# x transposed by DMA, and every segment 320 matmuls long, in a recurrent-memory attention and gMLP kernel

## The chip, the cores and the metric

The kernel runs on one core of one Trainium2 chip. What counts is the time of one execution on the device, in microseconds (us). Times of the kernel are medians of several executions; the views of the profile come from one profiled execution.

## What is computed

Two blocks follow one another. Block A is attention over 64 segments of 32 rows, in order: each segment's input is 8 memory rows and 32 rows of the normalised x, and the first 8 output rows are the memory of the next segment. Block B is a gMLP block over all 2048 rows. Cut to what matters here:

```python
for s in range(n_seg):                       # 64 segments, one after the other
    xs = x[:, s*32:(s+1)*32, :]              # x is layernorm(A_x), 2048 x 512
    h = concatenate([mem, xs], axis=1)       # 8 + 32 rows
    q, k, v = h @ Wq, h @ Wk, h @ Wv         # 32 heads of 128
    p = softmax(mask(q @ k.T * scale))
    o = (p @ v) @ Wo
    mem = o[:, :8, :]                        # goes on to segment s + 1
    outs.append(o[:, 8:, :])
h = A_x + concatenate(outs)
z = gelu(layernorm(h) @ w_in)                # 2048 x 1792
g = w_sp @ layernorm(z[..., 896:]) + b_sp    # mixes the rows
out = h + (z[..., :896] * g) @ w_out
```

All inputs are bfloat16.

## The kernel before

**How it is written.** Each instruction is added in Python to one of five lists, one for each engine: `pe` (TensorE, PE below), `act` (ScalarE), `dve` (VectorE), `pool` (GpSimd), and `sp` (SyncE, which issues DMAs). An engine works through its list in order. The writer names what an instruction reads and writes, and the class `Emitter` puts in the waits between engines; a wait that is already implied by an earlier one is left out. One wait rides on an instruction; where there are two, the second stands in the queue as an instruction of its own. An access to a bank of PSUM is tracked bank by bank, so a write to a bank waits until the other engines have read what stood there.

**A pair.** Each matmul is two instructions of PE's queue, the load of its weights and the matmul itself; below this is a pair. Nearly all of block A is written as groups of four pairs that fill the four 32-column strips of the array side by side (`tile_position=(0, 32 * c)`).

**Two parts of a segment.** PE doesn't multiply 40 rows at once. The recurrent part, 24 rows of x and the 8 of memory, goes through segment by segment. The last 8 rows of x of each segment don't fit into the 32 columns; they are worked out ahead of time for 16 segments together (a chunk): their Q and K columns (`qkx_mm`) and their V (`vx_mm`, whose result is stored to memory and loaded segment by segment as `Vx`). Their output projection is done for four segments together (`WoX_mm`, 8 pairs for each quarter), and scattered into rows by `WoX_scatter`.

**The loop over segments** (lines 975 to 1139), with `rb = s // 4`, the row block of 128 rows, and `j4 = s % 4`. What PE does from the first score matmul of a segment to that of the next one, in pairs:

- scores of the first half of the heads (20), V of the first half (16), scores of the second half (20), sums of the softmax and V of the second half in turns (8, 12, 8, 4)
- a column group `xs` of 16 pairs for a later chunk (lines 1056 to 1061): until segment 47 Q, K or V columns, from segment 49 on a part of z for block B
- an atom of a V group: four pairs of a group of 16, from the stock `gv` (class `Gap`; `gv.pour(n)` gives up to n atoms, and ends early where a group is complete, so that its result can be copied out)
- P times V (20 + 20), which needs the normalised E of DVE
- `WoX_mm` of the row block before (8, from the second row block on)
- Wo (56), the first half of the memory output `mem_out(s, 0)` (8), the rest of Wo (8)
- where j4 is 0 the residual rows (`F_group`, 4), where it is 3 `WoX_scatter` (4), where it is 2 the transposes of x described below (16), where it is 1 the second half of WoX, or an atom
- Q and K of the next segment: 8 pairs that need the first half of the memory columns, `mem_out(s, 1)` (8), and the other 72

The memory columns come to the next segment over PE (`mem_out`), ACT (line 724 copies them from bank `GB` = 1 into `hT`) and back to PE (`QK`). In `pour`, the number of atoms for a segment comes from `nC`: 3 in the first row block, then 2 for j4 = 1 and 1 otherwise.

**x.** `load_x(rb + 2, 0)` loads a row block two row blocks ahead, for j4 = 0; `ln_inplace(0)` normalises it for j4 = 1; for j4 = 2 PE transposes it with 16 matmuls against the identity (`xT_cols`, line 392) into PSUM bank `FBK`, and ACT copies it into a ring of 12 segment slots, `hT` (`ring_copy`, line 402), from which Q, K and V read. Segment 3 transposes 128 rows more, for the last chunk.

**Other queues.** SP issues, in its order, the loads of x and of the residual, the stores of V columns, `load_vx(s + 2)` (Vx for two segments later), pieces of the transposed w_sp (`wT_piece`, in odd segments) and, from segment 47 on, the transposes by DMA of the rows that block B needs (`xn2T_dma`, line 788). At the end of segment 47 it issues the load of one half of w_in. POOL copies the extra columns of Q (`qx_copy`, line 559, for the next segment), multiplies the small part of E (line 630), copies columns of cT (`cTx_copy`) and works out the reciprocal roots of the layernorms (`rstd`). `S_half` waits for POOL's `qx_copy` and for DVE at its first pair, so there the second wait stands by itself in PE's queue, in three segments of four.

**Start.** Before the first real work PE runs 78 small matmuls on a constant tile of ones (line 826) and some larger ones (`warm`).

## Time and profile before

| what | us |
|---|---|
| time, median of 3 executions | 849.89 (849.73 to 851.56) |
| the profiled execution | 849.45 |
| its span, from the first to the last instruction | 847.7 |
| PE busy in it | 832.2 |
| ACT busy | 498.4 |
| DVE busy | 493.3 |
| POOL busy | 154.8 |

How to read it: PE's busy time is the union of its matmuls, whose ends are modelled and which overlap (the mean matmul of 512 columns in line 534 is given 380 ns, though 3072 of them take 185.2 us together). A PE that is busy may therefore still stand behind its best pace; the pace is read from the starts of successive rows. In rows of the timeline the columns are start, length from the first start to the last end, engine, line, operation, shapes, count, and in brackets the idle time before with what ended it; "issue" means that nothing the profile shows was waited for. Rows of the chain of waits have start, length and what ran. Rows that group instructions have busy time, mean ns of one, and the idle time before. Rows of a window have its bounds, its length, then the busy time and count of PE, PEld (weight loads), DVE, ACT and POOL, the granted PE clock (1.00 throughout), the DMA share and GB/s; a window's count includes matmuls that are still in flight at its start.

### The profile page before, as it was taken

How to read it: one execution, taken by the hardware profiler on the slowest of the kernel's cores; microseconds unless marked ns; L12 is line 12 of the kernel's file. 1: busy time of each engine (PE TensorE's matmuls, PEld its weight loads, DVE VectorE, ACT ScalarE, POOL GpSimd, SP SyncE). 2: the span in 40 equal slices, each digit the busy share in tenths (PEclk: the TensorE clock that was granted, in tenths of full speed). 3: DMA queues.
4: the chain of work that ended last, by engine and by line, in shares of the span. 5: the costliest groups of instructions: out<-in, count | busy, mean ns of one | idle time of the engine just before them, and what ended most of it. 6: DMA issues, size and time to landing. Idle time of an engine off the chain costs nothing.

```text
span 847.7 us, 48032 instructions
## 1 busy us (share of the span) xinstructions
PE 832.2 (98%) x22034; PEld 475.2 (56%) x22034; DVE 493.3 (58%) x1175; ACT 498.4 (59%) x1419; POOL 154.8 (18%) x409
## 2 busy tenths in 40 slices
PE   8999999999999999999999999999999999999997
PEld 8655555555555555555556556555655544444443
DVE  4446556666565656565656566566656576553443
ACT  3456677767676777667777777666666676300000
POOL 5212111112211111111222121112211123200000
PEclk9999999999999999999999999999999999999999
DMA  9972222120301130213212130523332389023101
GB/s 330 386 216 87 70 45 62 52 78 21 82 29 44 57 79 29 66 59 61 65 30 77 30 79 26 122 70 77 70 82 59 70 268 305 1 99 100 44 13 46
DMA packets 95359, 76.03 MB, mean 90 GB/s; under 512 B 46184, under 2 KB 80624, under 8 KB 95152
## 3 DMA queue, kind: packets, MB, share of 16 engines
q1 hardware_dynamic: 93232, 70.09, 28.8%
q8 instruction: 174, 2.85, 1.5%
q10 hardware_dynamic: 1648, 2.49, 0.9%
q0 software_dynamic: 272, 0.33, 0.1%
q14 instruction: 33, 0.27, 0.1%
HBM read 41.75 MB, written 20.91 MB: 74 GB/s over the span
## 4 chain that ended last, share of the span: by engine, by line
PE 93%; DMA 3%; SPq 2%; issue 1%; ACT 0%; DVE 0%; POOL 0%; POOLq 0%
PE f_ps L534 27%; PE f_ps L701 14%; PE f_ps L640 13%; PE f_ps L1206 11%; PE f_ps L422 4%; PE f_ps L746 4%; PE f_ps L1301 3%; PE f_ps L472 3%; PE f_ps L665 2%; PE f_ps L797 2%; PE f_ps L1199 2%; PE f_ps L445 2%; DMA f_arena<-in_A_Wo_dram 1%; PE f_ps L585 1%; SPq L884 1%; PE f_ps L606 1%
## 5 line engine op out<-in xcount | busy, mean ns | idle before, releaser
L534 PE MATMUL f_ps<-f_arena,f_hT 128*32 128x512 bf16 (+1 forms) x5120 | 241.3, 337 | 0.9 <-ACT f_part L713 0.5
L534 PEld LDWEIGHTS f_ps<-f_arena,f_hT 128*32 128x32 bf16 x5120 | 117.2, 96 | 99.7 <-ACT f_hT L724 34.2
L545 ACT ACTIVATE f_Tst<-f_ps 128x512 bf16<-128x512 f32 (+2 forms) x320 | 146.7, 511 | 32.8 <-PE f_ps L534 32.1
L640 PE MATMUL f_ps<-f_arena,f_hT 128*32 128x512 bf16 x2048 | 138.7, 379 | 0.0
L701 PE MATMUL f_ps<-f_arena,f_cT 128*32 128x256 bf16 x4096 | 134.6, 273 | 1.2 <-issue 0.5
L630 POOL TENSOR_TENSOR f_E_sb<-f_R_sb,f_E_sb 128x64 bf16<-128x64 f32 x128 | 47.2, 369 | 387.1 <-ACT f_R_sb L622 386.5
L701 PEld LDWEIGHTS f_ps<-f_arena,f_cT 128*32 128x32 bf16 x4096 | 95.8, 95 | 31.8 <-ACT f_cT L687 8.8
L652 DVE TENSOR_SCALAR f_V_sb<-f_ps 128x512 bf16<-128x512 f32 (+1 forms) x128 | 71.4, 558 | 54.2 <-PE f_ps L640 54.2
L1206 PE MATMUL f_ps<-f_arena 128*128 128x512 bf16 x448 | 100.6, 379 | 0.1
L553 DVE STREAM_TRANSPOSE f_QT<-f_Tst 128x256 uint32<-128x256 uint32 x128 | 57.1, 446 | 65.6 <-ACT f_Tst L545 60.9
L689 DVE TENSOR_SCALAR f_cT<-f_ps 128x320 bf16<-128x320 f32 x128 | 56.8, 486 | 40.7 <-PE f_ps L671 40.7
L713 ACT ACTIVATE f_part<-f_ps 128x256 bf16<-128x256 f32 x128 | 49.2, 384 | 41.0 <-PE f_ps L701 38.9
L1206 PEld LDWEIGHTS f_ps<-f_arena 128*128 128x128 bf16 x448 | 43.6, 98 | 52.7 <-DMA f_arena<-wT_d 0.3
L687 ACT ACTIVATE f_cT<-f_ps 128x160 bf16<-128x160 f32 (+1 forms) x192 | 53.8, 346 | 26.5 <-PE f_ps L671 26.5
L599 ACT ACTIVATE f_E_sb<-f_ps 128x224 bf16<-128x224 f32 x128 | 45.4, 355 | 39.2 <-PE f_ps L611 39.2
L553 DVE STREAM_TRANSPOSE f_KT<-f_Tst 128x256 uint32<-128x256 uint32 (+2 forms) x192 | 60.7, 342 | 5.7 <-ACT f_Tst L545 3.0
L640 PEld LDWEIGHTS f_ps<-f_arena,f_hT 128*32 128x32 bf16 x2048 | 46.0, 95 | 20.0
L724 ACT ACTIVATE f_hT<-f_ps 128x16 bf16<-128x16 f32 x126 | 23.2, 184 | 47.7 <-PE f_ps L721 47.7
L571 DVE CAST f_ps<-f_mask 128x224 f32<-128x224 bf16 x80 | 29.8, 372 | 35.3 <-ACT f_hT L402 32.4
L1212 DVE TENSOR_TENSOR f_arena<-f_ps,f_arena 128x512 f32<-128x512 f32 x28 | 19.3, 689 | 52.7 <-PE f_ps L1206 52.7
L622 ACT ACTIVATE f_R_sb<-f_R_sb 128x160 f32<-128x160 f32 x128 | 43.1, 337 | 4.4 <-ACT f_Vs L484 0.4
L746 PE MATMUL f_ps<-f_arena,f_cTx 128*32 128x512 bf16 x512 | 41.5, 383 | 0.0
(128 smaller groups left out, 1142.0 us busy)
## 6 DMA issues: line engine op xcount, KB each, us to landing
wT_d<-f_wst SPq DMA_DIRECT2D x32, 256.0 KB, 2.3
f_arena<-wT_d SPq DMA_DIRECT2D x32, 256.0 KB, 5.0
f_arena<-in_A_Wv_dram SPq DMA_DIRECT2D x4, 1024.0 KB, 13.1
f_arena<-in_A_Wk_dram SPq DMA_DIRECT2D x4, 1024.0 KB
f_arena<-in_A_Wo_dram SPq DMA_DIRECT2D x4, 1024.0 KB, 12.3
f_Vx<-vext_d SPq DMA_DIRECT2D x62, 64.0 KB
vext_d<-f_Vs SPq DMA_DIRECT2D x22, 128.0 KB, 2.7
zp_d<-f_Vs SPq DMA_DIRECT2D x20, 112.0 KB, 1.7
```

The lines of the kernel that those rows point to most:

```text
L534: pe(lambda e, dc=dc, c=c, rhs=rhs: e.matmul(ps[32 * c:32 * c + 32, bank, 0:32 * nh], lhsT=hT[:, sl, dc, :], rhs=rhs, start=(dc == 0), sto ...
L545: act(lambda e: e.activation(out=st_.rearrange("p (hp i r) -> p hp i r", i=32, r=2), in_=ps[:, bank, 0:64 * np_].rearrange("p (hp r i) -> ...
L553: dve(lambda e: e.transpose(out=dst, in_=src), reads=tok, writes=[(nm, b, k) for k in halves(b, p0, np_)])
L630: pool(lambda e: e.tensor_tensor(out=ev, in0=rv, in1=ev, op=ALU.mult), reads=[("R", b), ("Ex", b)], writes=[("Ex", b)])
L640: pe(lambda e, dc=dc, c=c, c0=c0: e.matmul(ps[32 * c:32 * c + 32, bank, 0:w], lhsT=hT[:, sl, dc, :], rhs=w_v[:, dc, c0:c0 + w], start=(dc ...
L652: dve(lambda e: e.tensor_scalar(out=dst, in0=src, scalar1=VSC, scalar2=None, op0=ALU.mult), reads=[PB(bank)], writes=tok)
L687: act(lambda e: e.activation(out=dst, in_=src, func=ACT.Copy, scale=UNSC), reads=[PB(bank)], writes=tok)
L689: dve(lambda e: e.tensor_scalar(out=dst, in0=src, scalar1=UNSC, scalar2=None, op0=ALU.mult), reads=[PB(bank)], writes=tok)
L701: pe(lambda e, h=h, g=g, i=i, b=b, c=c: e.matmul(ps[32 * g:32 * g + 32, bank, 0:d1 - d0], lhsT=cTh[:, i, 8:40], rhs=w_o[:, h, d0:d1], star ...
L713: act(lambda e: e.activation(out=part[:, s % 8, d0:d1], in_=ps[:, bank, 0:d1 - d0], func=ACT.Copy), reads=[PB(bank)], writes=[("part", s % ...
L746: pe(lambda e, h=h, g=g, i=8 * qr + bg: e.matmul(ps[32 * g:32 * g + 32, WXB, :], lhsT=cTx[:, rb % 2, i, :], rhs=w_o[:, h, :], start=(i < 4 ...
L1206: pe(lambda e: e.matmul(ps[:, bank, 0:TB], lhsT=z2[:, sc, fb * 128:(fb + 1) * 128], rhs=wTb[tb % 2][:, :, sc, :], start=first, stop=last), ...
```

## The change

- **x by DMA.** For j4 = 1 SP stores the normalised row block to memory (`xl_store`), for j4 = 2 it loads it back transposed (`xl_transpose`) into a free half of `xo` (first three row blocks) or `xn`, and for j4 = 3 POOL copies it into the ring (`xl_copy`). The 16 matmuls and ACT's copy go, in 14 segments. Segment 3 keeps its own transposes.
- **Constant matmuls.** `pad(4)` is four matmuls of 8 columns on the tile of ones. They stand where a segment pours no atom: ahead of P times V (from the second row block on), and ahead of QK for j4 = 1 and 2.
- **Atoms.** `n_pre` gives one atom ahead of P times V for j4 = 0 and 3, and in the first four row blocks for all; `n_post` gives two between P times V and Wo in the first row block and in segments 50 and 51. For j4 = 1 and 2 (and in segment 0) one more atom stands ahead of QK, if the segment has completed no group. `WoX_mm` is no longer split.
- **Segments 48 to 51.** WoX of quarters 0 and 1 takes the place of the missing column group of segment 48; quarter 2 follows in 48, quarter 3 in 49; 50 and 51 have none.
- **The wait for POOL** is moved from the first score pair to the last pair of the last QK piece, where it is the only wait.
- **Constants at the beginning:** 82 instead of 78.
- `S_mask(0)` goes to DVE where a V group was completed, otherwise to ACT (before: to DVE for j4 = 2).

```diff
+    def xl_buf(rb):
+        return (xo, ("xo", 1)) if rb < 3 else (xn, ("xn", 1))
+
+    def xl_store(rb):
+        sp(lambda e: e.dma_start(xl_d[rb], xn[:, 0, :]), reads=[("xn", 0)], writes=[("xld", rb)])
+
+    def xl_transpose(rb):
+        t, tok = xl_buf(rb)
+        sp(lambda e: e.dma_start_transpose(out=t[:, 1, :].rearrange("p (dc t) -> p dc t", dc=DC), in_=xl_d[rb]),
+           reads=[("xld", rb)], writes=[tok])
+
+    def xl_copy(rb):
+        t, tok = xl_buf(rb)
+        src = t[:, 1, :].rearrange("p (dc s c) -> p s dc c", dc=DC, s=4, c=SEG)[:, :, :, 0:XM]
+        s0 = slot(4 * rb)
+        pool(lambda e: e.tensor_copy(out=hT[:, s0:s0 + 4, :, M:32], in_=src), reads=[tok], writes=[("hTx", rb % 3)])
+
+    def pad(n):
+        for i in range(n):
+            pe(lambda e, c=i % 4: e.matmul(ps[32 * c:32 * c + 32, GB, 504:512], lhsT=onesrc[:, 0:32], rhs=onesrc[:, 0:8], start=True,
+                                           stop=True, tile_position=(0, 32 * c)), reads=["onesrc"], writes=[PB(GB)])
...
-    def QK(s, piece, dcs=range(DC)):
+    def QK(s, piece, dcs=range(DC), after=()):
...
+                   after=after if (dc, c) == (DC - 1, 3) else ())
...
-    for i in range(78):
+    for i in range(82):
...
-    def nC(s, rb, j4):
-        if rb == 0:
-            return 3
-        return 2 if j4 == 1 else 1
+    wxp = {3 * CK: ((0, 1), (2,)), 3 * CK + 1: ((), (3,)), 3 * CK + 2: ((), ()), 3 * CK + 3: ((), ())}
+
+    def n_pre(s, rb, j4):
+        if s > 3 * CK:
+            return int(j4 in (0, 3) or s == 3 * CK + 5)
+        return int(j4 in (0, 3) or rb < 4)
+
+    def n_post(s, rb, j4):
+        return 2 if rb == 0 or s in (3 * CK + 2, 3 * CK + 3) else 0
...
-            QK(s, QKP[pi], range(2, DC) if pi < 2 else range(DC))
+            QK(s, QKP[pi], range(2, DC) if pi < 2 else range(DC), [em.last_w[("QTe", 0)]] if s > 0 and pi == 4 else ())
...
+        if s in wxp:
+            xs = [lambda qr=qr: WoX_mm(rb - 1, qr) for qr in wxp[s][0]]
...
-        n0, two = len(gv.atoms), j4 == 1 and rb > 0 and len(gv.atoms) > 1
-        pv = gv.pour(1) if nC(s, rb, j4) else []
+        n0 = len(gv.atoms)
+        pv = gv.pour(n_pre(s, rb, j4))
+        if rb > 0 and len(gv.atoms) == n0:
+            pad(4)
...
         if not pv:
-            pv = gv.pour(nC(s, rb, j4) - 1)
-        turn = two and n0 - len(gv.atoms) == 1
-        wx = range(4) if two and not turn else range(8)
-        late += [] if turn else [lambda f=f: f("act") for f in pv]
-        if rb > 0:
-            WoX_mm(rb - 1, j4, wx)
+            pv = gv.pour(n_post(s, rb, j4))
+        late += [lambda f=f: f("act") for f in pv]
+        if s in wxp:
+            for qr in wxp[s][1]:
+                WoX_mm(rb - 1, qr)
+        elif rb > 0:
+            WoX_mm(rb - 1, j4)
...
-        if turn:
-            pv[0]("dve")
...
+        if j4 == 3 and rb + 2 < RB:
+            xl_copy(rb + 2)
...
-        if j4 == 2 and 2 <= rb + 2 < RB:
-            xT_cols(0, FBK)
-            late.append(lambda: ring_copy(rb + 2, FBK, ps))
...
-        if rb > 0 and len(wx) == 4:
-            WoX_mm(rb - 1, j4, range(4, 8))
-        if turn or (not pv and (s < 2 or (rb >= RB - 2 and j4 == 2))):
-            late += [lambda f=f: f("act") for f in gv.pour(1)]
+        if j4 in (1, 2) or s == 0:
+            n0 = len(gv.atoms)
+            if not pv:
+                pv = gv.pour(1)
+                late += [lambda f=f: f("act") for f in pv]
+            if len(gv.atoms) == n0:
+                pad(4)
...
-            S_mask(0, "dve" if j4 == 2 or s == 3 else "act")
+            S_mask(0, "dve" if pv or s == 3 else "act")
...
+        if j4 == 1 and rb + 2 < RB:
+            xl_store(rb + 2)
+        if j4 == 2 and rb + 2 < RB:
+            xl_transpose(rb + 2)
```

More of the change, by code (lines that the diff above doesn't have):

```diff
@@ L259, in fast_path @@
     zp_d = nc.dram_tensor("zp_d", [RB, 128, FH], BF, kind="Internal").ap()
+    xl_d = nc.dram_tensor("xl_d", [RB, 128, D], BF, kind="Internal").ap()
     h_d = nc.dram_tensor("h_d", [RB, 128, D], BF, kind="Internal").ap()
@@ L535, in QK @@
                                                            start=(dc == 0), stop=(dc == DC - 1), tile_position=(0, 32 * c)),
-                   reads=[("hTx", (s // 4) % 3), ("hTm", s, dc // 2), ("W", mi, 2 * b), ("W", mi, 2 * b + 1)], writes=[PB(bank)])
+                   reads=[("hTx", (s // 4) % 3), ("hTm", s, dc // 2), ("W", mi, 2 * b), ("W", mi, 2 * b + 1)], writes=[PB(bank)],
+                   after=after if (dc, c) == (DC - 1, 3) else ())
     def halves(b, p0, np_):
@@ L1056, in fast_path @@
         xs = gx.pop(0) if gx else []
+        if s in wxp:
+            xs = [lambda qr=qr: WoX_mm(rb - 1, qr) for qr in wxp[s][0]]
         if s > 3 * CK and zcol:
             zr, zh = zcol.pop(0)
-            xs = [lambda dc=dc: zp_mm(zr, zh, XB, (dc,)) for dc in range(DC)] + [lambda: zp_evac(zr, zh, XB, "dve")]
+            xs += [lambda dc=dc: zp_mm(zr, zh, XB, (dc,)) for dc in range(DC)] + [lambda: zp_evac(zr, zh, XB, "dve")]
         for f in xs[:4]:
```

## The prediction

> **What bounds the kernel now.** First the page: busy times, the packets that carry instructions, and the chain that ended last.
>
> ```profile
> span 847.7 us, 48032 instructions
> ...
> PE 832.2 (98%) x22034; PEld 475.2 (56%) x22034; DVE 493.3 (58%) x1175; ACT 498.4 (59%) x1419; POOL 154.8 (18%) x409
> ...
> q8 instruction: 174, 2.85, 1.5%
> ...
> PE 93%; DMA 3%; SPq 2%; issue 1%; ACT 0%; DVE 0%; POOL 0%; POOLq 0%
> ```
>
> PE is busy for 98% of the span and carries 93% of the chain: what leaves PE's queue can shorten the run, what leaves ACT or DVE can't by itself. PE's queue holds 22034 pairs of weight load and matmul, 44068 instructions; 2.85 MB over them is 65 bytes each, and 2.85 MB over 174 packets is 16.4 KB, so a packet of queue q8 brings some 253 instructions: a block of about 127 pairs.
>
> Next the chain in order of time, which starts the long QK run (72 matmuls) once in every segment.
>
> ```profile
> 1.55 6.88 DMA f_arena<-in_A_Wq_dram
> ...
> 55.14 3.11 PE f_ps L534 x72
> ...
> 85.05 3.11 PE f_ps L534 x72
> ...
> 114.95 3.11 PE f_ps L534 x72
> ...
> 215.73 3.11 PE f_ps L534 x72
> ...
> 226.34 3.08 PE f_ps L534 x72
> ...
> 547.45 3.11 PE f_ps L534 x72
> ...
> 557.29 3.11 PE f_ps L534 x72
> ...
> 675.48 3.11 PE f_ps L534 x72
> ```
>
> Then whole segments, each from the first score matmul to the next one's. Columns: length, then PE, PEld, DVE, ACT, POOL busy with counts.
>
> ```profile
> 269.11:279.08 9.97, 9.97 (x344) 5.92 (x336) 5.38 (x15) 7.54 (x23) 1.54 (x4) 1.00 0.07 21
> 490.23:500.04 9.81, 9.81 (x327) 5.69 (x321) 6.00 (x16) 7.19 (x22) 1.54 (x4) 1.00 0.13 40
> 500.04:509.86 9.82, 9.75 (x322) 5.63 (x316) 6.15 (x17) 7.08 (x22) 2.33 (x6) 1.00 0.52 124
> 509.86:519.66 9.80, 9.80 (x339) 5.90 (x332) 5.38 (x15) 7.20 (x22) 1.54 (x4) 1.00 0.02 5
> ```
>
> The first is segment 22, with a V atom; the others are 44, 45 and 46, after the V atoms have run out. A segment takes 9.97 with atoms, 9.81 without, and 9.84 (547.45 to 557.29) in the last stage. The 62 segments from 55.14 to 675.48 last 620.34. By the code's counts 38 of them have V atoms (s = 1 to 38), 10 have none (39 to 48), 14 lie in the last stage: 38 x 9.97 + 10 x 9.81 + 14 x 9.84 = 614.7. The other **5.6 us** are irregular stops, such as the 10.61 from 215.73 to 226.34.
>
> What these stops are, the timeline and counted windows tell. The windows run from one stop to another (first three) and over the last block before a stop (the others).
>
> ```profile
> 124.96:165.05 40.09, 39.86 (x1279) 23.59 (x1278) 24.09 (x62) 28.73 (x85) 7.73 (x20) 1.00 0.22 54
> 165.05:225.05 60.00, 59.69 (x1920) 34.49 (x1918) 38.40 (x96) 42.77 (x127) 11.48 (x30) 1.00 0.21 55
> 225.05:316.15 91.10, 90.76 (x2941) 52.50 (x2941) 54.58 (x138) 65.51 (x193) 17.79 (x46) 1.00 0.22 59
> 221.06:224.58 3.52, 3.52 (x132) 2.21 (x125) 2.62 (x7) 2.53 (x8) 1.54 (x4) 1.00 0.47 79
> 392.98:396.30 3.32, 3.32 (x134) 2.21 (x128) 1.80 (x6) 2.13 (x8) 1.23 (x3) 1.00 0.23 84
> ```
>
> ```profile
> 225.24 0.40 PE L701 MATMUL f_ps<-f_arena,f_cT 128*32 128x256 bf16 x8 [0.50 <-issue]
> ```
>
> Between stops lie 1279, 1920 and 2941 matmuls: 10, 15 and 23 times 127.9. So PE stops where an instruction block ends, for no semaphore ("issue"), 0.5 us in this row, and only behind blocks that it got through in 3.3 to 3.5 us. The mean block takes 9.97 / 320 x 128 = 4.0, and blocks that long pass without a stop: the next block is not always there after 3.5 us.
>
> [...]
>
> **The change, part by part.** Costs inside a segment come from the timeline of segments 22 (first five rows) and 45.
>
> ```profile
> 272.48 0.27 PE L665 MATMUL f_ps<-f_E_sb,f_V_sb 32*128 32x40 bf16 x16
> ...
> 272.88 0.61 PE L746 MATMUL f_ps<-f_arena,f_cTx 128*32 128x512 bf16 x8
> 273.33 1.82 PE L701 MATMUL f_ps<-f_arena,f_cT 128*32 128x256 bf16 x56
> ...
> 275.26 0.40 PE L392 MATMUL f_ps<-f_ident,f_xn 128*32 128x128 bf16 x16
> 275.50 0.61 PE L534 MATMUL f_ps<-f_arena,f_hT 128*32 128x512 bf16 x8
> ```
>
> ```profile
> 503.20 0.27 PE L665 MATMUL f_ps<-f_E_sb,f_V_sb 32*128 32x40 bf16 x16
> ...
> 503.70 0.62 PE L746 MATMUL f_ps<-f_arena,f_cTx 128*32 128x512 bf16 x8
> ...
> 505.82 0.39 PE L701 MATMUL f_ps<-f_arena,f_cT 128*32 128x256 bf16 x8
> 506.28 0.62 PE L534 MATMUL f_ps<-f_arena,f_hT 128*32 128x512 bf16 x8
> ```
>
> *Transposes off PE.* Sixteen matmuls of line 392 hold PE from 275.26 to 275.50, 0.24 us, in 14 segments: 3.4 us of PE work removed. It isn't all gain, since they covered the wait for the memory columns. Eight matmuls of 512 take 0.45 (272.88 to 273.33), so an atom of four takes 0.22, and in segments with j4 = 1 or 2 a late atom now stands where the transposes or half of WoX stood: cover of the same size. What leaves is the early atom, replaced by four pads. Without it PE reaches PV before the normalised E: segment 45 takes 0.50 for the PV rows, segment 22 takes 0.40, so 0.10 of the 0.22 comes back as a wait. The result is the 9.81 measured without early atoms. Such segments are j4 = 1 and 2 of s = 17 to 38: 12 x 0.16 = **-1.9**. The V atoms end at s = 38 as before (12 through s = 2 instead of 11, 15 instead of 12 through s = 3, then six and later four a row block instead of five). In s = 3 the two more atoms fill the wait for cT that nothing covers in the first row block: 0, at worst +0.4, two atoms. In the last stage 54, 57, 58, 61 and 62 lose the early atom: 5 x (9.84 - 9.81) = **-0.15**.
>
> *Pads.* The trace has the like at line 827.
>
> ```profile
> L827 PE MATMUL f_ps<-f_onesrc 128*32 128x8 bf16 x78 | 0.8, 173 | 1.1 <-POOL f_onesrc L326 1.1
> ```
>
> 0.8 / 78 is 10 ns, so four take 0.04. Early pads lie in the 0.10 of waiting before PV: 0 (29 x 0.04 = +1.2 if that cover fails). Late pads write bank 1, which ACT's copy of the memory columns still reads, so they wait for the same copy as QK behind them and add their 0.04 on the path; and segments 42 and 46 lose the transposes as cover, which costs what segment 45 shows, 0.02. Four segments (41, 42, 45, 46): **+0.2**, between 0 and 0.4. The four constants more at the beginning, 0.04, lie in the wait for Wq (first row of the chain above): 0.
>
> *The way by DMA.* Each row block adds a store and a transpose on SP, and its copy moves from ACT to POOL.
>
> ```profile
> f_xn<-in_A_x_dram SPq DMA_DIRECT2D x16, 128.0 KB, 3.4
> ...
> f_arena<-xn_d SPq DMA_TRANSPOSE x10, 3.1
> ```
>
> ```profile
> L559 POOL COPY f_QT<-f_arena 128x256 bf16<-128x256 bf16 x64 | 25.4, 398 | 4.0
> ...
> L402 ACT ACTIVATE f_hT<-f_ps 128x384 bf16<-128x384 f32 x14 | 6.8, 488 | 0.0
> ```
>
> Store and transpose land in about 3 us and have a segment each; behind them on SP stand the loads of Vx, due two segments later. POOL, 18% busy, waits at the copy; 384 elements by the 398 ns for 256 make 0.6 us (estimate). Behind it stand rstd, used in the next segment, and the small E product, half a segment away. The slots are needed four segments on. ACT's 0.49 goes, off the path. All 0; were the transpose a whole segment late, POOL would hold E and each of 14 copies could cost some us, which nothing here suggests.
>
> *Segment 48* has no column group now, and waits at PV.
>
> ```profile
> 532.59 0.27 PE L665 MATMUL f_ps<-f_E_sb,f_V_sb 32*128 32x40 bf16 x16 [0.77 <-DVE f_E_sb L626]
> ...
> 537.44 0.21 PE L721 MATMUL f_ps<-f_G_sb,f_part 128*32 128x8 bf16 x7 [1.15 <-issue]
> ```
>
> The moved WoX (16 pairs, 0.9) fills the 0.77; segments 49 to 51, which lose WoX, get V atoms: 0 in sum. The stop of 1.15 at the block's end follows the load of w_in2, which the code issues at the end of segment 47.
>
> *Block ends.* With 320 pairs and the POOL wait folded into QK's last matmul, a segment is 2.5 blocks, so block ends return every two segments. Which places? Up to s = 4 the counts cancel (4 more constants, -12 in s = 2, +8 in s = 3), so segments 4 to 6 of the kernel before show them: from 85.05 to 114.95 they take 29.90, three times 9.97, without a stop. Counted on from the stops they are pairs 70 and 198 of even and 6, 134 and 262 of odd segments. Pair 6 is in the first scores, 134 in PV's second half, six pairs after it begins. That is the one short block in five:
>
> ```profile
> 500.07:503.47 3.40, 3.40 (x143) 1.84 (x134) 2.42 (x7) 2.55 (x9) 0.71 (x2) 1.00 0.50 125
> ```
>
> 3.40 without the early atom, 0.1 more with it (by the rows above PV starts 3.37 into segment 22 and 3.16 into 45, which then waits 0.10 longer); the other four share two segments less this, 19.6 - 3.4 = 16.2, about 4 each. Before, ends drift by 12 pairs or more in four segments and pass through every place. Walking them through the rows, I find some 45 blocks under 3.6 us, and the 5.6 less 1.3 for segment 48 (the 1.15 and what its pipeline hides), spread over them are 0.10 each. The changed kernel has 30 (s = 5 to 63): at 0.08, a little less since segments 4 to 6 ran free here, 2.4. Segment 48 is now cut at pair 198 instead of 221, nearer the w_in2 load: 1.3 to 2.5, taken as 1.9. So 4.3 for 5.6: **-1.3**, between -4.3 (only 1.3 left) and +5.3 (0.3 at each of the 30, and 1.9).
>
> **Sum:** -1.9 - 0.15 + 0.2 - 1.3 = -3.15. The profiled execution took 849.45 for a span of 847.7; that gives 846.3, and the median of 849.89 lies 0.44 above it: **846.7 us**.
>
> **Rivals.** *No block stops at all* but 1.3 in segment 48: for it, segments 4 to 6 without a stop; against it, the stops behind blocks of 3.5. -1.85 - 4.3 = -6.15: 843.7. *Placing does nothing*, and 5.6 us of stops remain: for it, stops also depend on what DMA carries; against it, they follow short blocks alone. 849.89 - 1.85: 848.0. [...] *The locked place is a bad one* (slower): every odd segment ends its short block just too early, and the traffic that delays one fetch comes round as regularly. For it, 3.40 is as short as the blocks that stopped at 3.32 and 3.52; against it, segments 4 to 6 passed these very ends at full pace. At 0.3 each: 30 x 0.3 + 1.9 - 5.6 - 1.85 = +3.45, 853.3. It decides from 0.185 a block on.
>
> **How the numbers follow.** Forecast 0.43, no stops 0.15, placing does nothing 0.22, bad place 0.20. A difference below 0.2% (1.7 us) can't be told from none here, so faster is below 848.2, slower above 851.6. Faster: 0.40 of the forecast, 0.15, and 0.10 of the case in which placing does nothing, 0.65, put at 0.64; slower: the worse part of the last case, 0.16; same 0.20. The forecast's own range is 845 to 848; with the other cases 843.0 to 851.5.
>
> **What would show it.** Right: segments 17 to 38 with j4 = 1 or 2 at 9.81; rows without a releaser only at pair 134 of odd segments and in segment 48; no wait of POOL for a DMA. Wrong: stops in nearly every odd segment, or at pairs 70, 198 and 262; j4 = 1 and 2 still at 9.97; PV waits above 0.1; POOL's copy ending after the segment's end.

## The result, and the profile after

| | us, median | ratio to before, 95% interval |
|---|---|---|
| before, run beside it (22 executions) | 851.26 (848.37 to 853.33) | |
| after (22 executions) | 852.88 (850.08 to 865.86) | 1.0022 [1.0012, 1.0032] |

The change costs 0.1 to 0.3%. The profiled execution of the changed kernel took 852.87 us, near its median; that of the kernel before (849.45) lies 1.8 us below the median of its 22, so the two profiles differ by more than the kernels do. The 865.86 is one execution at a lower granted clock (0.949), and it enters no ratio.

The page of the changed kernel answers to the first lines shown of the page before:

```profile
span 851.1 us, 47843 instructions
...
PE 835.6 (98%) x21940; PEld 484.4 (57%) x21946; DVE 492.2 (58%) x1175; ACT 497.2 (58%) x1405; POOL 162.1 (19%) x423
...
q8 instruction: 173, 2.83, 1.5%
```

PE runs 88 pairs fewer (its weight loads fall from 22034 to 21946; of the matmuls six are missing in this trace), and the span is 3.4 us longer. The chain in order of time gives the 62 segments again, by the start of the long QK run (line 557 now):

```profile
55.83 3.11 PE f_ps L557 x72
...
678.24 3.11 PE f_ps L557 x72
```

That is 622.41 where the kernel before took 620.34. Did the segments get cheaper? Windows of segments 22 and 34, both with j4 = 2, and of segments 44 and 58:

```profile
269.60:279.41 9.81, 9.81 (x332) 5.87 (x325) 5.28 (x15) 7.30 (x22) 1.53 (x4) 1.00 0.08 22
389.61:399.41 9.80, 9.80 (x330) 5.79 (x324) 5.27 (x15) 7.29 (x22) 1.53 (x4) 1.00 0.07 20
489.79:499.60 9.81, 9.81 (x331) 5.79 (x324) 6.00 (x16) 7.17 (x22) 1.54 (x4) 1.00 0.14 40
630.76:640.57 9.81, 9.81 (x333) 5.85 (x326) 5.08 (x14) 6.61 (x21) 1.53 (x4) 1.00 0.13 35
```

They did: segment 22 took 9.97 before. With the forecast's own prices (26 segments at 9.97, 22 at 9.81, then 5 at 9.81 and 9 at 9.84) the 62 segments would take 612.65 without stops. So the stops are 622.41 - 612.65 = **9.8 us, where 4.3 were forecast and the kernel before had 5.6**. Three windows show where: segments 4 to 47, segment 48, segments 49 to 62.

```profile
88.74:529.51 440.77, 439.36 (x14092) 260.57 (x14084) 270.18 (x682) 314.05 (x921) 90.67 (x231) 1.00 0.25 61
529.51:540.30 10.79, 10.07 (x332) 5.92 (x325) 5.56 (x15) 6.67 (x21) 1.54 (x4) 1.00 0.49 138
540.30:681.18 140.88, 139.16 (x4491) 83.55 (x4485) 84.33 (x211) 93.62 (x281) 26.51 (x68) 1.00 0.35 76
```

Without stops these would be 23 x 9.97 + 21 x 9.81 = 435.3, then 9.81, then 137.6; so 5.5, 1.0 and 3.3 us are lost. A stop looks like this in the timeline of segment 33:

```profile
379.12 0.27 PE L609 MATMUL f_ps<-f_QT,f_KT 128*32 128x40 bf16 x16
...
382.52 0.22 PE L689 MATMUL f_ps<-f_E_sb,f_V_sb 32*128 32x40 bf16 x6
383.25 0.24 PE L689 MATMUL f_ps<-f_E_sb,f_V_sb 32*128 32x40 bf16 x10 [0.51 <-issue]
```

PE stands six pairs into PV's second half, the forecast's pair 134, for no semaphore. Many stops are shorter and spread over overlapping matmuls, so that a sum over segments shows more of them than the list of waits does (9.8 us above, where the waits of PE that name no releaser come to 4.4 over the whole run). Two such sums: first six pairs of segments with j4 = 1 and 2 (from 17, 21 ... 37 on; 6 x 19.62 = 117.7 without stops), then five pairs with j4 = 3 and 0 (from 19, 23 ... 35 on; 5 x 19.94 = 99.7).

```profile
sum 119.97, PE 119.39 PEld 72.64 DVE 68.84 ACT 86.53 POOL 23.24; mean PE 19.90 PEld 12.11 DVE 11.47 ACT 14.42 POOL 3.87
```

```profile
sum 100.34, PE 100.34 PEld 58.81 DVE 65.50 ACT 70.85 POOL 21.85; mean PE 20.07 PEld 11.76 DVE 13.10 ACT 14.17 POOL 4.37
```

2.3 us are lost in the first kind and 0.6 in the second, though both kinds have the same block ends and a piece of w_sp in their odd segment. (PE's own busy sum rises with the stops, to 119.39 in the first kind, because ends are modelled.) Three questions follow. Is it the place of the block ends? Is it what the queues carry there? And why does j4 = 1 lose where j4 = 3 doesn't?

### The profile page after: what moved, and what is told of

Its sections match the earlier page's. It is cut to its first block, busy times and chain, and to the rows that moved or that the text cites. A ratio compares the mean times of both kernels' runs of the same rounds, so it can differ in the third digit from the quotient of the medians.

```text
span 851.1 us, 47843 instructions
## 1 busy us (share of the span) xinstructions
PE 835.6 (98%) x21940; PEld 484.4 (57%) x21946; DVE 492.2 (58%) x1175; ACT 497.2 (58%) x1405; POOL 162.1 (19%) x423
## 4 chain that ended last, share of the span: by engine, by line
PE 93%; DMA 3%; SPq 2%; issue 1%; DVE 0%; ACT 0%
PE f_ps L557 27%; PE f_ps L725 14%; PE f_ps L664 13%; PE f_ps L1243 11%; PE f_ps L445 4%; PE f_ps L770 4%; PE f_ps L689 3%; PE f_ps L1338 3%; PE f_ps L495 2%; PE f_ps L1236 2%; PE f_ps L821 2%; PE f_ps L468 2%; PE f_ps L609 1%; DMA f_arena<-in_A_Wo_dram 1%; SPq L908 1%; PE f_ps L630 1%
## 5 line engine op out<-in xcount | busy, mean ns | idle before, releaser
L557 PEld LDWEIGHTS f_ps<-f_arena,f_hT 128*32 128x32 bf16 x5120 | 121.0, 96 | 98.7 <-ACT f_hT L748 37.1
L664 PE MATMUL f_ps<-f_arena,f_hT 128*32 128x512 bf16 x2048 | 142.3, 379 | 0.0
L664 PEld LDWEIGHTS f_ps<-f_arena,f_hT 128*32 128x32 bf16 x2048 | 50.3, 95 | 20.5 <-issue 3.2
L445 PE MATMUL f_ps<-f_arena,f_hTe 128*32 128x512 bf16 x640 | 43.0, 379 | 0.0
L609 PEld LDWEIGHTS f_ps<-f_QT,f_KT 128*32 128x32 bf16 x2048 | 31.5, 95 | 16.5 <-DVE f_KT L577 16.4
```

What stands on the lines that cost most here:

```text
L445: pe(lambda e, c=c, rhs=rhs: e.matmul(ps[32 * c:32 * c + 32, bank, :], lhsT=hTe[:, ck, dc, 32 * sg:32 * sg + 32], rhs=rhs, start=(dc == 0) ...
L557: pe(lambda e, dc=dc, c=c, rhs=rhs: e.matmul(ps[32 * c:32 * c + 32, bank, 0:32 * nh], lhsT=hT[:, sl, dc, :], rhs=rhs, start=(dc == 0), sto ...
L664: pe(lambda e, dc=dc, c=c, c0=c0: e.matmul(ps[32 * c:32 * c + 32, bank, 0:w], lhsT=hT[:, sl, dc, :], rhs=w_v[:, dc, c0:c0 + w], start=(dc ...
```

## Experiments

"Stops" below are worked out as above, from the profile of each kernel: the three windows less 435.3, 9.81 and 137.6. One profile is one execution, and executions of one kernel spread by 3 us and more, so the stops show where time goes in that one and don't add up to the ratios; these are over 5 to 22 executions. A ratio is to the kernel before run beside each one, whose median lay between 849.35 and 852.19; medians of different rows can't be compared.

| kernel | median us | ratio, interval | stops in 4 to 47 | in 48 | in 49 to 62 |
|---|---|---|---|---|---|
| after | 852.88 | 1.0022 [1.0012, 1.0032] | 5.5 | 1.0 | 3.3 |
| no_x_dma | 853.93 | 1.0034 [1.0015, 1.0053] | 6.4 | 1.0 | 3.8 |
| const_98 | 850.71 | 1.0014 [0.9998, 1.0031] | 3.5 | 4.3 | 1.9 |
| const_114 | 848.15 | 0.9975 [0.9953, 0.9997] | 0.9 | 1.8 | 0.7 |
| const_146 | 849.61 | 1.0000 [0.9988, 1.0013] | 1.4 | 4.1 | 0.1 |
| wt_even | 848.69 | 0.9975 [0.9956, 0.9994] | 0.5 | 3.9 | 0.8 |
| wt_even_49 | 846.74 | 0.9979 [0.9964, 0.9994] | 0.5 | 1.2 | 1.3 |
| wt_even_49_114 | 848.64 | 0.9987 [0.9974, 1.0000] | 0.5 | 1.3 | 0.6 |
| w_in2_late | 846.98 | 0.9983 [0.9972, 0.9994] | 0.3 | 0.0 | 2.9 |
| pieces_j3 | 852.30 | 1.0040 [1.0025, 1.0054] | 1.1 | 1.0 | 0.0 |
| piece_held | 850.70 | 0.9984 [0.9967, 1.0001] | 2.5 | 4.4 | 2.1 |

**Is it the added DMA traffic?** no_x_dma takes the 14 stores and transposes of x out of the changed kernel; before_x_dma adds them, unused, to the kernel before.

```diff
--- no_x_dma, against after
-        return (xo, ("xo", 1)) if rb < 3 else (xn, ("xn", 1))
+        return (xn, ("xn", 1))
...
-        if j4 == 1 and rb + 2 < RB:
-            xl_store(rb + 2)
-        if j4 == 2 and rb + 2 < RB:
-            xl_transpose(rb + 2)
--- before_x_dma, against before
+        if j4 == 1 and rb + 2 < RB:
+            xl_store(rb + 2)
+        if j4 == 2 and rb + 2 < RB:
+            xl_transpose(rb + 2)
```

> The changed kernel without the 14 stores and 14 transposes of x; POOL copies stale rows into the ring, so from the third row block on the segments work on wrong x. PE's queue is the same, pair for pair. Theory 'traffic' (the added DMA packets delay the instruction blocks): the stops fall back from about 10 us to 5 or less, ratio to before 0.996 or below. Theory 'place' (the block ends stand at a bad place): the stops stay, ratio 1.001 to 1.003.

> The kernel before with the same 14 stores and 14 transposes added, their result unused. Traffic: more stops, ratio 1.003 to 1.006. Place: the drifting block ends stay as good as they were, ratio within 0.001 of 1.

Measured: 1.0034 [1.0015, 1.0053] without the traffic, and 1.0000 [0.9980, 1.0020] with it in the kernel before. Traffic as such costs the kernel before nothing that can be seen (within 0.2%), and without it the changed kernel gained nothing: its ratio is at or above after's, and the stops are no fewer. But they have moved. The same two sums, j4 = 1 and 2 and then j4 = 3 and 0:

```profile
sum 120.05, PE 119.38 PEld 73.30 DVE 68.84 ACT 85.95 POOL 23.18; mean PE 19.90 PEld 12.22 DVE 11.47 ACT 14.33 POOL 3.86
```

```profile
sum 102.26, PE 100.89 PEld 59.55 DVE 65.46 ACT 71.13 POOL 21.81; mean PE 20.18 PEld 11.91 DVE 13.09 ACT 14.23 POOL 4.36
```

Segments with j4 = 3 and 0 now lose 102.26 - 99.7 = 2.6 us where the changed kernel loses 0.6. Over all segments from 4 to 46 those with j4 = 1 lose 2.0 (2.1 in the changed kernel), with j4 = 2 0.8 (2.5), with j4 = 3 3.0 (0.2). That none of the theories had foreseen; the reason for j4 = 3 is in the phase, below.

**Is it the place of the block ends?** Only the number of constants at the beginning is altered. Each adds a pair ahead of the work, so every block end comes one pair earlier in it: with 98 at pairs 118 and 246 of odd and 54, 182 and 310 of even segments, with 114 at 102 and 230 of odd and 38, 166 and 294 of even ones. Where an expectation has them later, the direction was mistaken (64 pairs come to the same either way, as a block has 128 pairs, 127.9 by the counts between the stops of the kernel before).

```diff
-    for i in range(82):
+    for i in range(114):
```

> The changed kernel with 114 constants in place of 82: all block ends 32 pairs later in the code, that is at pairs 102 and 230 of even and 38, 166 and 294 of odd segments less 64, with blocks of other lengths. Place: the time moves by at least 0.3% either way. Traffic: ratio stays at 1.001 to 1.003.

> 98 constants: the block ends 16 pairs later than in the changed kernel, at pairs 22, 150 and 278 of odd and 86 and 214 of even segments; pieces in odd segments. The block that ends in PV's second half or just behind it (134 to 150) now has 16 pairs of the long ones (WoX and Wo) more and 16 short score pairs less: about 1 us longer, 4.0 to 4.4 us in place of 3.3. Theory 'place' and theory 'meeting' both: fewer stops in odd segments, about as with 114 constants, ratio 0.9975 (0.995 to 1.000). If the phase of the end against the pieces' packets decides and not the block's length: anything between 0.997 and 1.003, without order in the constants.

> 146 constants in place of 82: every block end lies 64 pairs later than in the changed kernel, which is one segment on, so that the pairs 6, 134 and 262 are now met in even segments and 70 and 198 in odd ones. The same places in the segment, but the other parity: the pieces of w_sp stay in odd segments. Theory 'place' (what counts is where in the segment a block ends and how short the block is): the same stops with the parities exchanged, about 10 us, and a time like the changed kernel's, ratio to the kernel before 1.002 (1.000 to 1.004). Theory 'meeting' (a block stops when its end of 3.3 us meets the packets of a w_sp piece): the short block now lies in segments without a piece, as in the kernel with the pieces in even segments: stops of 2 to 5 us outside segment 48, ratio 0.997 (0.994 to 0.999). Segment 48 keeps 1 to 2 us by either.

Measured: 32 pairs more give 0.9975 [0.9953, 0.9997], with 3.4 us of stops in place of 9.8; 16 more 1.0014 [0.9998, 1.0031]; 64 more 1.0000 [0.9988, 1.0013]. So moving the block ends alone changes the time, for 32 constants of 10 ns each. The expectation for const_98 was wrong, and not only in the direction: it looked for one longer block and not for the next short one. A stop of it, in segment 25 (first score matmul at 299.67), and SP's row for the piece's store there:

```profile
302.83 0.27 PE L689 MATMUL f_ps<-f_E_sb,f_V_sb 32*128 32x40 bf16 x16
...
306.33 0.20 PE L745 MATMUL f_ps<-f_G_sb,f_part 128*32 128x8 bf16 x6
307.05 0.18 PE L745 MATMUL f_ps<-f_G_sb,f_part 128*32 128x8 bf16 x2 [0.52 <-issue]
```

```profile
302.60 0.33 SPq L842 DMA_DIRECT2D wT_d<-f_wst  x1
```

PE stops at pair 246. That block began at 118, ten pairs into PV (302.9), and ran for 3.6 us; what SP issues there is not the transpose of the piece but the store that follows it. The next packet of q8 begins 4.71 us into the segment, where it begins 4.23 and 4.27 into segments 23 and 27, which lose nothing. 16 pairs exchanged one short block at a bad moment for another.

**Is it the meeting with the pieces of w_sp?** const_146 already spoke for it: the same places with the parity exchanged, and outside segment 48 stops of 1.5 us where the changed kernel has 8.8. Its ratio of 1.0000 doesn't decide: it lies above the range of 'meeting' (0.994 to 0.999) and at the lower end of that of 'place' (1.000 to 1.004), and segment 48 lost 4.1 where both had 1 to 2. Its three windows:

```profile
89.23:525.91 436.68, 435.98 (x14093) 254.08 (x14085) 270.01 (x682) 312.74 (x921) 90.47 (x231) 1.00 0.23 61
525.91:539.77 13.86, 11.52 (x329) 6.92 (x324) 5.54 (x15) 6.65 (x21) 1.54 (x4) 0.88 0.37 109
539.77:677.44 137.67, 137.64 (x4492) 81.00 (x4484) 84.26 (x211) 93.03 (x281) 26.43 (x68) 1.00 0.32 78
```

The other way round, the block ends stay and the pieces move to even segments (wt_even), and the one that then coincides with the load of w_in2 in segment 48 goes to 49 (wt_even_49):

```diff
-        if s % 2 == 1 and s // 2 < NWT:
+        if s % 2 == 0 and s // 2 < NWT:                 # wt_even
+        if s == 49 or s % 2 == 0 and s != 48:           # wt_even_49
             wT_piece(s // 2)
```

> The changed kernel with the w_sp transposes issued in even segments in place of odd ones, so that their packets meet the block ends of the other kind of segment; the computation is the same. Theory 'meeting' (the short block of odd segments always meets the w_sp packets): ratio falls to 0.996 to 0.998. Place alone or added traffic alone: 1.001 to 1.003 as before.

> The changed kernel with the pieces of w_sp in even segments, but the one of segment 48 in 49, apart from the load of w_in2. Theory 'meeting': segment 48 loses the 2.05 us stop and the slow clock behind it (3.94 us more than 9.8 in the profile of the kernel with all pieces in even segments) and keeps 1 to 1.5 us for the load of w_in2 alone; stops 3 to 5 us in all, time 846.2 (845 to 848), ratio 0.9945 (0.9925 to 0.9970). Theory 'place': the pieces don't matter, and ratio 1.002 (1.000 to 1.004). A third reading, that segment 48 stops for the load of w_in2 alone and the piece is innocent: as with all pieces even, ratio 0.9975.

> The kernel with the pieces in even segments (48's in 49) and 114 constants. If places and meetings are one cost (a block end of a short block that meets a piece), what one edit saves the other can't save again: 0.994 to 0.998, at best the sum of what the parities leave, stops of 2.5 to 5 us. If they are two costs that add, 0.9975 - 0.0047 (the step that each edit made from the changed kernel's 1.0022) = 0.993.

Measured: 0.9975 [0.9956, 0.9994] and 0.9979 [0.9964, 0.9994]; stops in segments 4 to 47 fall from 5.5 to 0.5 us in both. Meeting is confirmed, and 'place' alone, which asked for 1.002 and for unchanged stops in const_146, falls. wt_even_49 removed 2.7 of 3.9 us in segment 48, as expected in the profile, but its ratio of 0.9979 lies above the range given for it (0.9925 to 0.9970); by the ratio alone the third reading (0.9975) would do as well. wt_even_49_114 shows that the two edits don't add: 0.9987 [0.9974, 1.0000] where adding them would have given 0.993. They save the same stops, though 0.9987 lies above the 0.994 to 0.998 given for that too.

Does it hold without locked ends? before_even is the kernel before with the same pieces in even segments, before_110 the kernel before with 32 constants more.

> The kernel before with the pieces in even segments (48's in 49). Its block ends drift by 12 pairs or more in four segments and meet the pieces at any phase, in even segments as in odd ones. Theory 'locked meeting': no change, ratio 1.000 (0.998 to 1.002). If the pieces cost less in even segments for another reason (less on the queue there), it gains as the changed kernel did: 0.995 to 0.997.

> The kernel before with 110 constants in place of 78: the 32 pairs that took 0.47% off the changed kernel. Its block ends drift through all places and pass the pieces at every phase, so a shift moves which ends stop and not how many, by 'meeting' and 'place' alike: ratio 1.000 (0.998 to 1.002). If more constants were worth something by themselves (a warm clock, a later start of the stream), it would gain as the changed kernel did: 0.995.

Measured: before_even 0.9996 [0.9980, 1.0013], as expected: where block ends drift, the pieces cost the same in either parity. before_110 1.0018 [1.0006, 1.0030], within the range given but with an interval that lies above 1: 32 constants take nothing off by themselves, but the kernel before isn't wholly indifferent to the shift either.

**Why j4 = 1?** SP's queue in the timeline of the changed kernel around segment 25 (j4 = 1; first score matmul at 299.34) and segment 27 (j4 = 3; at 319.27):

```profile
297.38 0.43 SPq L764 DMA_DIRECT2D f_hbuf<-in_A_x_dram  x1
297.86 1.27 SPq L841 DMA_TRANSPOSE f_wst<-in_B_w_sp_dram  x1
...
318.13 1.22 SPq L414 DMA_TRANSPOSE f_xn<-xl_d  x1
319.39 1.32 SPq L841 DMA_TRANSPOSE f_wst<-in_B_w_sp_dram  x1
```

For j4 = 1 the piece is issued 1.48 us ahead of the segment, for j4 = 3 it is 0.12 behind its start, held up by the issue of the transpose of x. In no_x_dma that transpose is gone, the piece comes at 318.98, 1.14 ahead of segment 27's start at 320.12, and segments with j4 = 3 stop:

```profile
318.98 1.27 SPq L841 DMA_TRANSPOSE f_wst<-in_B_w_sp_dram  x1
```

What lies between is the block end at pair 6, in the first 0.2 us of the segment. By what follows, the packet of q8 that begins behind it brings the instructions that PE needs at pair 134. DMA in the first 1.26 us of segment 25 of the changed kernel, and of the same stretch of the kernel piece_held, described next:

```profile
DMA packets 596, 0.15 MB, mean 121 GB/s; under 512 B 596, under 2 KB 596, under 8 KB 596
## 3 DMA queue, kind: packets, MB, share of 16 engines
q1 hardware_dynamic: 596, 0.15, 79.8%
```

```profile
DMA packets 1, 0.02 MB, mean 13 GB/s; under 512 B 0, under 2 KB 0, under 8 KB 0
## 3 DMA queue, kind: packets, MB, share of 16 engines
q8 instruction: 1, 0.02, 4.8%
```

In the changed kernel 596 packets of the piece, all under 512 bytes, keep the DMA engines 80% busy, and no packet of q8 has begun. In piece_held the packet of q8 has the engines to itself: 4.8% of 16 engines over 1.26 us is 0.97 us.

The time of q8's first packet in each odd segment from 5 to 47 of the changed kernel, read from its trace, says the same for all of them. In eleven segments it begins 0.26 to 1.06 us behind the first score matmul, and these lose 0.03 us at most; in the other eleven it begins 1.16 to 1.54 us behind it, and these lose 0.03 to 0.68. Nine of the late ones are just the segments with j4 = 1 whose piece is issued 1.48 us ahead. The two with j4 = 1 that lose nothing, 5 and 13, have their piece 0.55 and 0.17 us ahead; the other two late ones are 19 and 35, for which no cause was looked for. Where PE then stops at pair 134, it goes on 1.2 to 1.6 us behind the end of the late packet: in segment 33 the packet runs from 380.66 to 381.68, and PE goes on at 383.25.

In piece_held only the piece of j4 = 1 waits, for the first score matmul of its own segment:

```diff
-        if s % 2 == 1 and s // 2 < NWT:
+        if j4 == 3:
             wT_piece(s // 2)
...
+        npe = len(em.by_eng["pe"])
         S_half(s, 0)
+        if j4 == 1:
+            wT_piece(s // 2, [em.by_eng["pe"][npe]])
```

> The changed kernel, in which the piece of w_sp in segments with j4 = 1 waits for the segment's first score matmul, and so is issued 0.1 to 0.3 us behind it (where the piece of j4 = 3 is issued without a wait) and not 0.2 to 1.5 us before it; the same segment, the same packets. Theory 'phase' (the piece's packets stand ahead of the fetch that the block end at pair 6 starts, and the short block runs out): of the 4.8 us that segments 4 to 46 with j4 = 1 and 2 lose in the profile of the changed kernel, less than 1.5 is left; ratio 0.998 (0.995 to 1.000). Theory 'presence' (a piece and the load of the h rows in one odd segment are too much whenever they come): 4 us or more stay there, ratio 1.002.

The sum over the six pairs with j4 = 1 and 2 is

```profile
sum 118.11, PE 118.11 PEld 71.40 DVE 68.80 ACT 85.93 POOL 23.23; mean PE 19.68 PEld 11.90 DVE 11.47 ACT 14.32 POOL 3.87
```

and the issue of segment 25's piece, whose first score matmul is at 296.85:

```profile
297.11 1.72 SPq L841 DMA_TRANSPOSE f_wst<-in_B_w_sp_dram  x1
```

0.4 us are left of 2.3 in these twelve segments; over 4 to 46 the j4 = 1 and 2 segments keep 1.5 of 4.6 (by the prices used here, 9.97 and 9.81; the expectation had 4.8), at the bound of the 1.5 expected. The same packets in the same segment, 1.7 us later: for j4 = 1, where 0.2 of 2.1 is left, it is the **phase**, not the presence. The ratio of 0.9984 [0.9967, 1.0001] agrees, though this profile happened to lose 4.4 us in segment 48.

The other 2.5 of the 4.6 lay in the segments with j4 = 2, which have no piece; 1.3 of that stayed. They stop elsewhere, at pair 70. Here are the second half of V and the beginning of PV in segment 22 of the changed kernel, which loses nothing (first score matmul at 269.60), and in segment 26 (309.25):

```profile
270.82 0.82 PE L664 MATMUL f_ps<-f_arena,f_hT 128*32 128x512 bf16 x12
...
272.76 0.27 PE L689 MATMUL f_ps<-f_E_sb,f_V_sb 32*128 32x40 bf16 x16
...
310.51 1.02 PE L664 MATMUL f_ps<-f_arena,f_hT 128*32 128x512 bf16 x10
...
312.64 0.27 PE L689 MATMUL f_ps<-f_E_sb,f_V_sb 32*128 32x40 bf16 x16
```

PV starts 3.16 into the one and 3.39 into the other. In all ten even segments from 4 to 46 that lose time, seven of them with j4 = 2, the matmul of pair 70 starts 1.63 to 1.83 us in; in the twelve that lose none it starts at 1.44 or 1.45. (Four of the ten, 10, 36, 38 and 42, come behind a stop at pair 262 of the segment before, which accounts for 0.1 us of this.) The fetch in question is the last of the odd segment, behind its pair 262. It begins 8.7 to 9.2 us into the nine segments with the early piece, and 7.7 to 8.4 into the same nine of wt_even, so a late fetch may hand its delay on. But that isn't all of it: three segments of piece_held have it at 8.6 to 9.0 though their first one was early, and without the store of x at the end of j4 = 1 (no_x_dma) the segments with j4 = 2 lose only 0.8. These two causes were not tested apart.

Doubling was tried before that: pieces_j3 puts two pieces into every segment with j4 = 3 and none into j4 = 1.

```diff
-        if s % 2 == 1 and s // 2 < NWT:
+        if j4 == 3:
+            wT_piece(s // 2 - 1)
             wT_piece(s // 2)
```

> The changed kernel with the same 32 pieces of w_sp, but two of them in every fourth segment (s = 3, 7, 11 ...) and none in segments 1, 5, 9 ... Block ends stay where they are. 'Meeting': within one kernel the odd segments part: those without a piece (1, 5, 9 ... 61) run nearly free, under 1 us in sum, and those with two lose as much as all odd ones in the changed kernel or more, 4 to 8 us; a piece may reach into the even segment behind it. Ratio 0.998 to 1.004. 'Place': both kinds of odd segments lose the same, 2 to 3 us each.

Half of it came: j4 = 1 ran free (117.72 for the six pairs). The other half failed: segments with two pieces didn't stop either (100.00 for the five pairs), which 'meeting' without a phase can't explain, for here the first piece comes behind the transpose of x, as before, and the second waits for the first. The loop is the best of all (stops 2.1), yet the kernel is slow, 1.0040. In its profile two pieces in the last segment hold up SP's loads for block B:

```profile
PE f_ps L1237 <- DMA f_arena<-in_B_w_in_dram: 3.3, 1, 3.3
```

The other executions were some 3 us slower than the profiled one (849.37); why is open.

**Segment 48** stops in every version of the table that loads w_in2 at the end of segment 47. w_in2_late is wt_even_49 with the load of w_in2 issued behind segment 48's PV.

```diff
+        if s == 3 * CK:
+            sp(lambda e: e.dma_start(w_in2, winr[:, :, FH:F]), writes=["w_in2"], after=[em.by_eng["pe"][-1]] + free0)
...
-            sp(lambda e: e.dma_start(w_in2, winr[:, :, FH:F]), writes=["w_in2"], after=free0)
```

> The kernel with the pieces in even segments (48's in 49), with the load of w_in2 (896 KB) issued behind segment 48's last PV matmul instead of at the end of segment 47. If the stop in segment 48 (1.2 us in that kernel, 4 us in those where it reached 2 us) is the load's, it goes, to under 0.4 us, and the time falls by 0.5 to 1: ratio 0.9970 (0.9950 to 0.9985). Against it: the fetch at pair 198 of segment 48 now meets the load, and the stop moves to the next block end, at pair 6 of segment 49, 0.5 to 1.5 us; or the matmuls of line 821 in segment 49 wait for the load.

Segment 48 took 9.81, no stop; two came in segment 49, the first at pair 6, the next block end:

```profile
535.16 0.25 PE L609 MATMUL f_ps<-f_QT,f_KT 128*32 128x40 bf16 x10 [1.28 <-issue]
...
539.28 0.24 PE L689 MATMUL f_ps<-f_E_sb,f_V_sb 32*128 32x40 bf16 x10 [0.58 <-issue]
```

The stop followed the load of 896 KB in either place: 1.2 us were lost in segment 48 of wt_even_49, and 1.28 and 0.58 in segment 49 here. That the load delays the fetch is read from the changed kernel, where the first packet of q8 begins 1.99 to 2.51 us into the twelve even segments from 4 to 46 that lose nothing, and 3.66 into segment 48. Nothing was gained: 0.9983 [0.9972, 0.9994].

**What beats both kernels:** wt_even, wt_even_49, const_114 and w_in2_late all do; their intervals end below 1 and overlap, so no one of them is shown to be the best.

## Why the prediction was wrong

The forecast was 846.7 with stops of 4.3; the time is 852.88. Of these 6.2 us 1.4 are the kernel before itself: the forecast began from 849.89, the median of three executions, and the 22 beside the changed kernel have 851.26. Against them the change costs 1.6 us (3.4 between the two profiles), where -3.15 was forecast. Point by point, by the profiles:

- **PE's work:** right. The segments without an early atom run at 9.80 to 9.81, the price was -1.9 and -0.15, and 622.41 - 620.34 = 2.07 is that (614.72 to 612.65) and the stops' 4.14 more (9.76 less 5.62).
- **Pads:** right within what can be seen. Line 425 has 132, 33 times four; segments 41, 42, 45 and 46 of wt_even_49, which have late pads and no stop, take 9.82 to 9.84 where 43 takes 9.80, so the four cost 0.1 and not 0.2. POOL's copy takes 507 ns each time, and POOL's waits name no DMA for it:

```profile
L425 PE MATMUL f_ps<-f_onesrc 128*32 128x8 bf16 x132 | 7.4, 170 | 0.3
```

```profile
L421 POOL COPY f_hT<-f_xn 128x384 bf16<-128x384 bf16 x13 | 6.6, 507 | 0.8
```

- **Segment 48:** 1.0 in the profile where 1.9 was taken: inside the 1.0 to 4.4 of the versions that load w_in2 at the same point.
- **Block ends, "at 0.08 each ... 2.4", "4.3 for 5.6":** this is the step that failed. Where the blocks end was right, and PE does stop at pair 134 of odd segments. Two things were wrong. One is the premise that only this short block can stop and "the other four", of about 4 us, are free: the ten even segments that stop at pair 70 do so behind blocks of 3.8 us, and about half of the 5.5 us lost in segments 4 to 47 lies in even segments. Stops at pairs 70, 198 and 262 stood among the prediction's own signs of being wrong. The other is the price. It was spread from the kernel before, where each end meets the pieces at another phase, and carried over to a kernel in which every fourth segment repeats one phase. There the 11 segments with j4 = 1 and the 11 with j4 = 2 between 4 and 46 lost 4.6 us, 0.2 each, and the other odd ones nearly nothing. With 8.8 us outside segment 48 in place of 2.4 the change turned from -3.15 to a loss; from 0.185 a block the forecast had said so itself, and 8.8 over its 30 blocks is 0.29.
- **The last stage**, segments 49 to 62, has 3.3 of these 8.8 us, 1.5 of them with j4 = 3 (segments 51 and 55). Which transfers the fetches meet there was not taken apart; with the block ends in the other parity (const_146) 0.1 is left.
- **The rival "the locked place is a bad one"** had the mechanism that the runs showed ("the traffic that delays one fetch comes round as regularly"), but not its places: it has every odd segment stop at pair 134. That its 853.3 comes so near to 852.88 is luck in part: it had 10.9 us of stops where the profile has 9.8, nothing of the 1.3 us outside the loop (below), and began from the lower 849.89. It had 0.20 because segments 4 to 6 of the kernel before passed these ends at full pace. Among those three only one, segment 5, has j4 = 1, and in the changed kernel too segment 5 passed: 98.71 to 108.68 is 9.97. One sample without a stop was read as a rule, and it was not even a sample of the phase that counts. SP's queue in the kernel before, ahead of segments 5 (first score matmul at 97.95) and 9 (138.19):

```profile
95.49 1.28 SPq L817 DMA_TRANSPOSE f_wst<-in_B_w_sp_dram  x1
...
136.70 1.27 SPq L817 DMA_TRANSPOSE f_wst<-in_B_w_sp_dram  x1
```

The piece of segment 5 is issued 2.46 us ahead, that of segment 9 1.49, and so are those of 13, 21, 37, 41 and 45 (1.48 or 1.49). This could have been read before.

- **The rival "placing does nothing"** fell too: most block ends do pass without a stop (of the segments from 4 to 47, 11 of the 22 odd ones lose 0.03 us at most, and 12 of the 22 even ones nothing), but 32 pairs of shift are worth 0.47% (1.0022 to 0.9975), 4 us.

The rest of the 3.4 us of span lies outside the loop: 0.69 before it (55.83 against 55.14) and 0.64 behind. The first score matmul of segment 1 comes at 57.8 to 59.8 in profiles of kernels with nearly the same code ahead of it, so no cause is claimed for it. Not tried: what the chip does if the pieces are left out altogether, since block B reads them.

## What to carry to other kernels

A stream that repeats in a whole number of half blocks (here 320 pairs, 2.5 blocks of 127.9) locked the instruction fetches to the loop: from segment 3 to 62 of the changed kernel each odd segment has the beginning of three packets of q8 and each even one of two. An unlucky phase was then paid in nearly every turn (nine of the eleven segments with j4 = 1 from 5 to 45 had the late packet, and 2.1 us were lost in the eleven), and a lucky one was nearly free (0.2 us in the segments with j4 = 3), so the price of a boundary couldn't be averaged from the kernel before, whose ends drift: 0.10 a short block there, 0.29 a block here. Look at the shorter blocks (here those of 3.4 to 3.8 us) and at what SP issues in the 1.5 us ahead of their start: a transfer of many small packets there (596 under 512 bytes in the first 1.26 us of segment 25) delayed the fetch, which began 1.32 us into that segment and 0.26 to 1.06 into the odd ones that lost nearly nothing. Moving such a transfer to the other segment was worth about 4 us here, where the work saved on PE was 2. And a shift of the whole stream by a few cheap matmuls is a probe that costs one number in the source.

## What the runs showed of the hardware

A long stop cost more than itself. In segment 48 of wt_even PE stands for 2.05 us, and the QK run behind it, 3.26 long elsewhere, takes 4.59:

```profile
532.14 0.61 PE L725 MATMUL f_ps<-f_arena,f_cT 128*32 128x256 bf16 x14 [2.05 <-issue]
...
533.87 4.59 PE L557 MATMUL f_ps<-f_arena,f_hT 128*32 128x512 bf16 x72
```

```profile
533.29:536.70 3.41, 3.41 (x44) 1.30 (x40) 1.27 (x3) 1.24 (x5) 0.00 (x0) 0.50 0.43 148
```

The granted clock (the third number from the end of the window's row) is 0.50 for 3.41 us and 1.00 before and after, so a stop of 2 us became a loss of 3.9. In const_114 a stop of 1.50 in the same segment left the clock at 1.00:

```profile
531.80 1.49 PE L725 MATMUL f_ps<-f_arena,f_cT 128*32 128x256 bf16 x46 [1.50 <-issue]
```

```profile
531.80:538.00 6.20, 6.20 (x190) 3.86 (x189) 3.01 (x8) 4.03 (x11) 0.00 (x0) 1.00 0.20 52
```

The stops of 2.3 to 2.7 us in const_146, const_98 and piece_held went the same way as wt_even's (0.50 for 3.4 us, and 4.1 to 4.4 lost). One of 1.95 us in segment 48 of before_even did not:

```profile
539.06 0.21 PE L721 MATMUL f_ps<-f_G_sb,f_part 128*32 128x8 bf16 x7 [1.95 <-issue]
```

```profile
539.06:542.50 3.44, 3.44 (x103) 2.04 (x107) 1.53 (x4) 2.50 (x7) 0.00 (x0) 1.00 0.67 120
```

So in segment 48 stops of up to 1.95 us left the clock at 1.00, and those from 2.05 on did not. It isn't a bound on idle time as such: near the start of wt_even_49_114 a wait of 1.95 us for the load of Wq, until 9.57, was followed by 3.4 us at 0.50 too.
